# Slot lists built on the chip by one-hot matmuls instead of slot writes, gate weights stored behind each row, long runs in the conversions

## The chip, the cores and the metric

The kernel runs on one core of one Trainium2 chip. The metric is the device time of one execution in microseconds; lower is better. The core has TensorE (matmuls, "PE" in the profile, its weight loads "PEld"), VectorE ("DVE"), ScalarE ("ACT"), GpSimd ("POOL"), SyncE ("SP", which issues most transfers) and 16 DMA engines.

## The reference

Attention with a window of 64 positions over 8 batches, 8 heads and 576 positions gives 4608 rows of 512 values. Each row goes to the best two of eight experts, with weights from a softmax over noisy logits. All in f32.

```python
rel = pos[:, None] - pos[None, :]
mask = (rel >= 0) & (rel < window)
attn = softmax(np.where(mask, scale * q @ k.T, -1e9))
x = (attn @ v) as rows [N, DM]
noisy = x @ w_gate + np.log1p(np.exp(x @ w_noise)) * noise
top2 = np.argpartition(-noisy, 2, axis=1)[:, :2]
top2_w = softmax over the two
for e in range(E):
    for k in range(2):
        m = top2[:, k] == e
        h = np.maximum(x[m] @ w1[e], 0.0)
        out[m] += top2_w[m, k, None] * (h @ w2[e])
```

## The kernel before, in words

The work has two stages, and the order of the instructions on each engine is the order in which the Python code issues them (no scheduler).

**Attention, 36 tiles of 128 rows** (the loop over `j`, line 719). It is a software pipeline: in pass `j` the scores of tile `j` are multiplied (L255), ScalarE and VectorE take the window and the maximum (L275, L283, L288), GpSimd subtracts the maximum (L289, once per tile), ScalarE takes the exponential of tile `j-1` (L293), TensorE transposes it (L301), VectorE masks it (L306), TensorE multiplies tile `j-2` with the values (L324), and ScalarE scales tile `j-3` (L343), which is then stored in DRAM as rows of `xrows` (L346). SyncE loads two to three tiles ahead.

**Routing** runs beside it. The tiles are grouped in five routes (`ROUTE`, 7, 7, 7, 6 and 9 tiles). For each, `route` (L407) issues some 35 small operations, a few per pass (`RATE`): softplus, noise, the best two experts as one-hot `oh`, running counts `cum`, and by two matmuls with a triangle and with ones (L463, L464) the rank of each row in its expert's list. The rank and the expert's base give a slot number `posi` (L477).

**Slot writes.** Each expert has a list in DRAM, `slots`, of `CAP` = 1216 entries and some for an overflow. An entry is a row number and a gate weight. For each tile and each of the two choices GpSimd issues one indirect DMA (L483) that writes 128 entries of 8 bytes to the slots of `posi`, behind a memset of one element; 72 in all. They wait in a queue `slots` and are taken from it one, then one or two, in each pass. Before, SyncE has filled the lists with numbers of empty rows (`load_pads`, L175).

**Experts.** Each expert's list is cut in chunks of 384, 448 and 384 rows. The first two chunks of expert 0 start before the routing is complete (`EARLY`). A chunk's list is read back (`load_list`, `load_lists`), GpSimd gathers its rows from `xrows` by indirect DMAs (L546), and `turn` (L564) makes the transposed operand in two parts, `xh` rounded and `xl` the rest. For expert 0 TensorE transposes; for the others the rows go out to DRAM (`turn_out`) and come back per tile in another order (`turn_in`), VectorE transposes blocks of 32 (L574), and ScalarE and VectorE convert (L584, L585), reading and writing with strides. Then `up` (L609): for each of eight column blocks, four times three matmuls of 384 or 448 columns; and `down` (L645): for each 128 rows, eight times three matmuls of 512 columns, one eviction by ScalarE, scaled by the gate weight of the list (L659), and one indirect DMA that adds the rows to the output (L640). In the 448-row chunk the last 64 rows take another path (L664 to L670). `spread` (L55) sets the side work (weight splits, gathers, the next `turn`) between the matmuls.

The chunk loop is at line 785. In its first pass the rest of the routing and of the slot writes runs beside the first up- and down-projection; `catch_up` (L793) makes sure that the gather of the second chunk has been issued before its `turn`. Up to sixteen steps of the first up-projection run already in the last passes of the attention loop (`ahead`).

The program stores zeros to the whole output beforehand (`zero_out`, L195), 37 transfers of 256 KB.

Of the kernel before, what the change touches and what calls it, by code (L numbers as in the profile page):

```python
# [65 lines left out]
def tile_kernel(ctx, tc, qT, kT, vx, vT, wgx, noise, w1, w2, out):  # L66
# [97 lines left out]

    pad_s = acon.tile([128, ROWS, 2], I32)
    pad_o = acon.tile([OVT, 128, 2], I32)
    nc.gpsimd.memset(pad_s, 0)
    nc.gpsimd.memset(pad_o, 0)
    nc.gpsimd.iota(pad_s[:, :, 0], pattern=[[0, ROWS]], base=0, channel_multiplier=1)
    nc.gpsimd.iota(pad_o[:, :, 0], pattern=[[1, 32], [32, 4]], base=0, channel_multiplier=0)  # L170
    pad_f = pad_s.rearrange("c t w -> c (t w)")
# [3 lines left out]
    def load_pads(q):  # L175
        if q == 0:
            nc.sync.dma_start(rows(L, LIST * 2, [[ROWS * 2, 128], [LIST * 2, E - 1], [1, ROWS * 2]]),
                              pad_f[:, None, :].to_broadcast([128, E - 1, ROWS * 2]))
            nc.sync.dma_start(rows(L, (LIST + ROWS * 128) * 2, [[2, TAIL], [LIST * 2, E - 1], [1, 2]]),
                              pad_f[:TAIL, None, :2].to_broadcast([TAIL, E - 1, 2]))  # L180
            return
        pad_t = pad_o.rearrange("k p c -> k (p c)")
        if q == 1:
            nc.sync.dma_start(rows(L, 0, [[256, CAP // 128], [1, 256]]), pad_t[:CAP // 128])
            nc.sync.dma_start(rows(L, CAP // 128 * 256, [[256, 1], [1, CAP % 128 * 2]]), pad_t[:1, :CAP % 128 * 2])
        else:
            nc.sync.dma_start(rows(L, CAP * 2, [[256, OVT], [LIST * 2, E], [1, 256]]),
                              pad_t[:, None, :].to_broadcast([OVT, E, 256]))

    REST = [lambda: nc.sync.dma_start(noise_sb, noise), lambda: nc.sync.dma_start(X[0:DUMP, :], zero),  # L190
            lambda: load_pads(0), lambda: load_pads(1), lambda: load_pads(2)]

    blank = list(range(N // 128 + 1))
# [734 lines left out]
```

## Time and profile before

| what | us |
|---|---|
| median of 3 runs | 1135.25 |
| lowest and highest | 1126.39, 1136.22 |
| the profiled execution | 1131.99 |
| its span, first to last instruction | 1130.2 |
| TensorE busy | 1044.2 |
| VectorE busy | 469.2 |
| ScalarE busy | 437.4 |
| GpSimd busy | 338.6 |

The profile is of one execution. Busy times are sums over instructions; matmuls are pipelined and their ends modelled, so a busy TensorE need not be at its peak. An idle time is put down to what ended it: a semaphore of another engine, a DMA, or "issue", when the profile shows nothing that the engine waited for; "remote" is a release that the profile finds on none of the core's engines. "PEclk", and the column behind the engines in the windows, are TensorE's granted clock as a share of 2.4 GHz.

### The profile page before, as it was taken

To read this page: it belongs to the slowest core of one execution; us is meant where nothing else is said; L and a number is where in the kernel's file an instruction comes from. 1 tells how busy PE (TensorE), PEld (TensorE's weight loads), DVE (VectorE), ACT (ScalarE), POOL (GpSimd) and SP (SyncE) were. 2 spreads that over 40 slices of the span, in tenths; PEclk is the share of its full clock that TensorE was granted. 3 is DMA by queue.
4 is the path that set the end of the run, shared out by engine and by line. 5 is a ranking of instruction groups with operands and counts; after the bars stand their busy time and mean duration, and the time that the engine had idled before them with its cause. 6 is when DMAs were issued, how large, how long until landed. Compare 5 with 4: busy or idle time off the path is not lost. (4 is left out here: it accounts for less than half of the span.)

```text
span 1130.2 us, 19820 instructions
## 1 busy us (share of the span) xinstructions
PE 1044.2 (92%) x8025; PEld 925.7 (82%) x8025; DVE 469.2 (42%) x943; ACT 437.4 (39%) x1011; POOL 338.6 (30%) x387
## 2 busy tenths in 40 slices
PE   9788888578599999999999999999999999999996
PEld 8777777366589888898988898889888988889895
DVE  5586556324114523452263325334533452354320
ACT  4776555332123432442253335323432343253320
POOL 4345444616412222122312123212221222322121
PEclk9898888879699999999999999999999999999998
DMA  9988889537414752564447445634762564244422
GB/s 321 314 300 206 214 198 307 150 133 235 123 27 112 221 146 33 173 195 103 81 130 200 103 108 146 180 81 98 203 172 40 157 205 113 44 99 112 102 33 31
DMA packets 104519, 168.07 MB, mean 149 GB/s; under 512 B 15096, under 2 KB 50530, under 8 KB 102626
## 3 DMA queue, kind: packets, MB, share of 16 engines
q1 hardware_dynamic: 84962, 126.78, 35.3%
q0 software_dynamic: 19456, 39.93, 19.2%
q8 instruction: 65, 1.06, 0.4%
q14 instruction: 36, 0.29, 0.1%
HBM read 109.54 MB, written 57.14 MB: 147 GB/s over the span
## 5 line engine op out<-in xcount | busy, mean ns | idle before, releaser
L625 PE MATMUL ps_u<-xh,w1h 128*128 128x384 f32 (+1 forms) x752 | 261.6, 348 | 15.6 <-ACT xh L584 15.1
L640 POOL DMA_INDIRECT out_dram<-yo,lts x70 | 112.1, 1602 | 543.9 <-ACT yo L659 430.7
L626 PE MATMUL ps_u<-xl,w1h 128*128 128x384 f32 (+1 forms) x752 | 261.4, 348 | 4.5 <-DVE xl L585 4.5
L627 PE MATMUL ps_u<-xh,w1l 128*128 128x384 f32 (+1 forms) x752 | 260.3, 346 | 0.0
L654 PE MATMUL ps_d<-w2h,hh 128*128 128x512 f32 x576 | 225.3, 391 | 0.0
L656 PE MATMUL ps_d<-w2h,hl 128*128 128x512 f32 x576 | 225.2, 391 | 0.0
L655 PE MATMUL ps_d<-w2l,hh 128*128 128x512 f32 x576 | 225.0, 391 | 0.0
L632 DVE SCALAR_TENSOR_TENSOR hl<-ps_u,hh 128x384 fp32r<-128x384 f32 x188 | 104.8, 557 | 275.9 <-ACT hh L631 261.6
L631 ACT ACTIVATE hh<-ps_u 128x384 fp32r<-128x384 f32 x188 | 92.5, 492 | 246.9 <-PE ps_u L627 236.5
L625 PEld LDWEIGHTS ps_u<-xh,w1h 128*128 128x128 f32 x752 | 141.9, 189 | 23.9 <-ACT xh L584 18.7
L626 PEld LDWEIGHTS ps_u<-xl,w1h 128*128 128x128 f32 x752 | 141.9, 189 | 11.2 <-DVE xl L585 6.7
L627 PEld LDWEIGHTS ps_u<-xh,w1l 128*128 128x128 f32 x752 | 141.9, 189 | 4.0
L585 DVE TENSOR_TENSOR xl<-xy,xh 128x512 fp32r<-128x512 f32 (+1 forms) x70 | 71.5, 1021 | 150.7 <-ACT xh L584 150.7
L654 PEld LDWEIGHTS ps_d<-w2h,hh 128*128 128x128 f32 x576 | 108.6, 189 | 23.8 <-issue 1.8
L656 PEld LDWEIGHTS ps_d<-w2h,hl 128*128 128x128 f32 x576 | 108.4, 188 | 22.8
L655 PEld LDWEIGHTS ps_d<-w2l,hh 128*128 128x128 f32 x576 | 108.5, 188 | 21.9
L659 ACT ACTIVATE yo<-ps_d,lts 128x512 f32<-128x512 f32 x63 | 43.4, 690 | 160.2 <-PE ps_d L656 119.1
L324 PE MATMUL ps_o<-vw,pt 64*64 64x85 f32 x2176 | 71.0, 257 | 29.4 <-issue 22.8
L584 ACT ACTIVATE xh<-xy 128x512 fp32r<-128x512 f32 (+1 forms) x70 | 74.4, 1063 | 56.1 <-DVE xy L574 56.1
L324 PEld LDWEIGHTS ps_o<-vw,pt 64*64 64x64 f32 x2176 | 58.7, 149 | 40.3 <-issue 32.1
L483 POOL DMA_INDIRECT slots<-val,posi x72 | 70.0, 972 | 20.1 <-issue 14.7
L546 POOL DMA_INDIRECT xg<-xrows,lts x70 | 69.3, 990 | 21.4 <-issue 20.1
(149 smaller groups left out, 991.3 us busy)
## 6 DMA issues: line engine op xcount, KB each, us to landing
xs<-xg SPq DMA_DIRECT2D x63, 256.0 KB
xg<-xs SPq DMA_DIRECT2D x63, 256.0 KB
w2s<-in_w_dram SPq DMA_DIRECT2D x7, 2048.0 KB
w1s<-in_w_dram SPq DMA_DIRECT2D x7, 2048.0 KB
vw<-in_vx_dram SPq DMA_DIRECT2D x36, 272.0 KB
out_dram<-zero SPq DMA_DIRECT2D x37, 256.0 KB
qc<-in_qT_dram SPq DMA_DIRECT2D x36, 256.0 KB
KW<-in_kT_dram SPq DMA_DIRECT2D x36, 256.0 KB
```

The costliest lines, as they stand in the source:

```text
L324: nc.tensor.matmul(PO[j][u * 64:u * 64 + 64, a, g * 2 + x, :], lhsT=pt[pa, w, u * 2 + g, x * 64:x * 64 + 64], rhs=v[pa, (i + w) % 2, :, u, ...
L584: nc.scalar.activation(h, cur[q], AF.Copy)
L585: nc.vector.tensor_tensor(l, cur[q], h.bitcast(F32), op=OP.subtract)
L625: nc.tensor.matmul(p[:, :n], lhsT=w1h[:, k, fs], rhs=xh[:, k, :n], start=(k == 0), stop=False)
L626: nc.tensor.matmul(p[:, :n], lhsT=w1h[:, k, fs], rhs=xl[:, k, :n], start=False, stop=False)
L627: nc.tensor.matmul(p[:, :n], lhsT=w1l[:, k, fs], rhs=xh[:, k, :n], start=False, stop=(k == KD - 1))
L631: nc.scalar.activation(h, p[:, :main], AF.Relu)
L632: nc.vector.scalar_tensor_tensor(l, p[:, :main], 0.0, h.bitcast(F32), op0=OP.max, op1=OP.subtract)
L640: nc.gpsimd.indirect_dma_start(out=out[:DUMP + seen.get((e, c), NT) * 128], out_offset=bass.IndirectOffsetOnAxis(ap=LT[e, c][q][:m, 0:1], ...
L654: nc.tensor.matmul(p, lhsT=hh[f][:, sl], rhs=w2h[:, f, :], start=(f == 0), stop=False)
L655: nc.tensor.matmul(p, lhsT=hh[f][:, sl], rhs=w2l[:, f, :], start=False, stop=False)
L656: nc.tensor.matmul(p, lhsT=hl[f][:, sl], rhs=w2h[:, f, :], start=False, stop=(f == KF - 1))
```

## The change

1. The slot writes go, and with them the prefilled lists. Instead a route now makes, for a pair of tiles and both choices, a one-hot of the slot number's low 7 bits over 128 lanes (`ha`, four compares of 128 columns on GpSimd, or on VectorE once the attention loop is over), a one-hot of its upper part over 80 list tiles (`hc`, one compare of 320 columns on VectorE), and the product of the latter with two values, the tile's number and the lane difference (`hb`, 640 columns on GpSimd). Four bf16 matmuls (128x160) add the two one-hots' products in PSUM: each row's number lands at its slot. VectorE adds the result to `SLOT`, which stays on the chip. Three VectorE operations turn it into the gather's and the store's row numbers (`lists`).
2. The gate weights are written behind each row: `xrows` is 528 wide instead of 512, and each route stores 16 weights per row with one DMA (L478). The gather brings them along, and one small copy per tile (`gate_of`) takes the weight of the expert.
3. The rows that come back from DRAM are read in another order, in four transfers per chunk (`turn_in`), so that transposes, `xh` and `xl` have runs of 32 elements instead of strides.
4. The half tile moves from the second to the third chunk (384, 384, 448). The empty entries of odd list tiles point to a second dump region of the output, and the stores of tiles with another parity in the same chunk don't wait for each other. The zeros come from a buffer of half the width. `RATE` is 6 operations a pass up to tile 15 and then 8. The pieces of side work in the first two chunks are set anew.

The diff, cut:

```diff
-CHUNKS = (384, 384 + TAIL, 384)
+CHUNKS = (384, 384, 384 + TAIL)
-XB = 8
+XB = 4
+XW = DM + 2 * E
-RATE = ((16, 6), (21, 8), (27, 6), (99, 8))
+RATE = ((16, 6), (99, 8))
...
-        yield lambda: nc.vector.tensor_tensor(oh, oh, rks[:, None, :, :].to_broadcast([128, 2, n, E]), op=OP.mult)
-        pos, posi = new("pos", [128, 2, n]), new("posi", [128, 2, n], I32, bufs=2)
-        yield lambda: nc.vector.tensor_reduce(pos, oh, op=OP.add, axis=AX.X)
-        yield lambda: nc.vector.tensor_copy(posi, pos)
...
-        def scatter(c2, q):
-            nc.gpsimd.memset(spacer, 0.0)
-            s = nc.gpsimd.indirect_dma_start(
...
-        slots.extend(lambda c2=c2, q=q: scatter(c2, q) for q in range(n) for c2 in range(2))
+        wd = new("wd", [128, n, 2, E])
+        for k in range(2):
+            yield lambda: nc.vector.tensor_tensor(wd[:, :, k], oh[:, k], w[:, k, :, 1:2].to_broadcast(sh), op=OP.mult)
+        yield lambda: nc.vector.tensor_tensor(wd[:, :, 0], wd[:, :, 0], wd[:, :, 1], op=OP.add)
+        yield lambda: nc.sync.dma_start(rows(X, (DUMP + j0 * 128) * XW + DM, [[XW, 128], [128 * XW, n], [1, 2 * E]]),
+                                        wd.rearrange("p q k e -> p q (k e)"))
...
+        yield lambda: nc.vector.tensor_scalar(hi, pos, 1.0 / 128, -0.498046875, op0=OP.mult, op1=OP.add)
+        yield lambda: nc.vector.tensor_scalar(hi, hi, 12582912.0, -12582912.0, op0=OP.add, op1=OP.add)
+        yield lambda: nc.vector.scalar_tensor_tensor(lo, hi, -128.0, pos, op0=OP.mult, op1=OP.add)
+        yield lambda: nc.vector.tensor_scalar(mul[:, :, :, 1], lo, -1.0, row, op0=OP.mult, op1=OP.add)
+        def at_lane(q, x):
...
+            for k in range(2):
+                (nc.gpsimd if j < NT else nc.vector).tensor_scalar(AB[q][0][:, 2 * x + k], lane, lo[:, q + x, k:k + 1], None, op0=OP.is_equal)
+        def at_tile(q, m):
...
+            nc.vector.tensor_tensor(h[:, :2 * m], t[:, None, :].to_broadcast([128, 2 * m, E * NQ]),
...
+        def at_both(q, m):
...
+            nc.gpsimd.tensor_tensor(AB[q][1][:, :2 * m], AB[q, 1][:, :2 * m, None, :].to_broadcast(sh),
...
+        def place(q, m):
+            a, b = AB[q]
+            for x in range(2 * m):
+                nc.tensor.matmul(SP, lhsT=a[:, x], rhs=b[:, x].rearrange("p v t -> p (v t)"),
+                                 start=(x == 0), stop=(x == 2 * m - 1))
+            v = SLOT.rearrange("p v e q -> p (v e q)")
+            nc.vector.tensor_tensor(v, v, SP, op=OP.add)
+        last = None
+        for q in range(0, n, 2):
+            m = min(2, n - q)
+            slots.append(lambda q=q, m=m: (at_tile(q, m), at_lane(q, 0)))
+            slots.append(lambda q=q, m=m, f=last: (m > 1 and at_lane(q, 1), f and f()))
+            slots.append(lambda q=q, m=m: at_both(q, m))
+            last = lambda q=q, m=m: place(q, m)
+        slots.extend([lambda: None, last])
...
+        yield lambda: nc.vector.scalar_tensor_tensor(ii[0], j, 128.0, p, op0=OP.mult, op1=OP.add)
+        yield lambda: nc.vector.scalar_tensor_tensor(m, j, 0.0, odd[:, es, qs], op0=OP.is_gt, op1=OP.max)
+        yield lambda: nc.vector.scalar_tensor_tensor(ii[1], m, float(DUMP), ii[0], op0=OP.mult, op1=OP.add)
...
         def turn_out(q, m):
-            b[q] = dram.tile([4, 128, 128], F32, name="xs", bufs=8)
...
+            nc.sync.dma_start(b[q * 128:q * 128 + m], XG[e, c, q][:m, :DM])
-        def turn_in(q, m):
...
+        def turn_in(g):
+            if g == 0:
+                XC[e, c] = exa.tile([128, WIDE // 32, 128], F32, name="xc", bufs=1)
+            nc.sync.dma_start(XC[e, c][32 * g:32 * g + 32, :CHUNKS[c] // 32],
+                              rows(b, g * 128, [[DM, 32], [32 * DM, CHUNKS[c] // 32], [1, 128]]))
...
-            h, l = (x[:, :, q * 128:q * 128 + m].rearrange("p k (c t) -> p k c t", c=32) for x in (xh, xl))
+            h, l = (x[:, :, q * 128:q * 128 + m].rearrange("p k (t c) -> p k t c", c=32) for x in (xh, xl))
...
+        for x in added.setdefault((e, 1 - (QS[c] + q) % 2), []):
+            tc.declare_no_dep(s.ins, x.ins, reason="distinct rows")
...
-                nc.scalar.activation(y, p, AF.Copy, scale=LT[e, c][q].bitcast(F32)[:, 1:2])
+                nc.scalar.activation(y, p, AF.Copy, scale=wt[:, q:q + 1])
```

How this stands on the engines is seen at two places. The first is GpSimd in the middle of the attention tiles, where the first route's slots are made: `t` is the softmax's tile, `spacer` the memset before each write, `posi` the slot numbers. Before:

```order
L289 TENSOR_TENSOR t<-t,mx 128x512
L482 MEMSET spacer 1x1
L483 DMA slots<-val_168,posi 38400x2
L482 MEMSET spacer 1x1
L483 DMA slots<-val_168,posi 38400x2
L289 TENSOR_TENSOR t<-t,mx 128x512
```

In the changed kernel, at the same tiles (`ha` the one-hot over lanes, `hb` the product, `mul` the two values):

```order
L269 TENSOR_TENSOR t<-t,mx 128x512
L494 TENSOR_SCALAR ha<-lane,lo 128x128 x2
L505 TENSOR_TENSOR hb<-hc,mul_175 128x640
L494 TENSOR_SCALAR ha<-lane,lo 128x128 x2
L269 TENSOR_TENSOR t<-t,mx 128x512
L494 TENSOR_SCALAR ha<-lane,lo 128x128 x2
L505 TENSOR_TENSOR hb<-hc,mul_175 128x640
L269 TENSOR_TENSOR t<-t,mx 128x512
```

Between two subtractions GpSimd now computes instead of issuing indirect DMAs.

The second place is TensorE in the down-projection of the first chunk, shortly before its end, where the second chunk's rows are transposed (`ps_d` is the projection's result, `ident,xg` a transpose). Before:

```order
L654 MATMUL ps_d<-w2h,hh 128x512
L655 MATMUL ps_d<-w2l,hh 128x512
L656 MATMUL ps_d<-w2h,hl 128x512
L579 MATMUL ps_u<-ident,xg 128x128 x4
L654 MATMUL ps_d<-w2h,hh 128x512
```

In the changed kernel (`ps_g<-hb,ha` are the matmuls of the one-hots):

```order
L713 MATMUL ps_d<-w2h,hl 128x512
L511 LDWEIGHTS ha
L511 MATMUL ps_g<-hb,ha 128x160
L511 LDWEIGHTS ha
L511 MATMUL ps_g<-hb,ha 128x160
L711 MATMUL ps_d<-w2h,hh 128x512
L712 MATMUL ps_d<-w2l,hh 128x512
L713 MATMUL ps_d<-w2h,hl 128x512
L625 MATMUL ps_u<-ident,xg 128x128 x4
```

TensorE has gained five groups of such matmuls here, each of which stands in front of the projection's next matmuls and waits for VectorE's and GpSimd's one-hots.

## Rows read from the trace of the kernel before

**Rows 1.** The page's 40 slices of the span, TensorE's busy tenths:

```profile
PE   9788888578599999999999999999999999999996
```

**Rows 2.** Windows: length, busy us (instructions) of PE, PEld, DVE, ACT, POOL, clock, DMA share, GB/s:

```profile
50.00:75.00 25.00, 20.33 (x533) 18.02 (x531) 20.00 (x53) 20.13 (x72) 12.20 (x15) 0.93 0.89 316
...
85.00:160.00 75.00, 61.54 (x1268) 53.59 (x1268) 47.64 (x134) 44.00 (x156) 40.19 (x66) 0.86 0.83 212
...
212.00:237.00 25.00, 9.62 (x63) 4.85 (x54) 0.60 (x5) 0.73 (x3) 16.86 (x33) 0.57 0.12 16
...
264.00:279.00 15.00, 15.00 (x69) 12.06 (x69) 2.04 (x8) 2.58 (x4) 11.46 (x20) 0.92 0.62 189
...
279.00:294.50 15.50, 0.42 (x2) 0.00 (x0) 0.97 (x2) 1.56 (x3) 10.52 (x18) 0.65 0.25 27
```

**Rows 3.** Timeline of GpSimd: start, us, instruction, idle time before it and releaser:

```profile
50.47 1.04 POOL L289 TENSOR_TENSOR t<-t,mx 128x512 f32<-128x512 f32 x1 [1.64 <-DVE mx L288]
...
94.84 1.05 POOL L289 TENSOR_TENSOR t<-t,mx 128x512 f32<-128x512 f32 x1
...
182.14 0.96 POOL L546 DMA_INDIRECT xg<-xrows,lt  x1 [0.30 <-issue]
...
207.37 1.04 POOL L289 TENSOR_TENSOR t<-t,mx 128x512 f32<-128x512 f32 x1 [3.17 <-DVE mx L288]
...
231.46 0.96 POOL L483 DMA_INDIRECT slots<-val,posi  x1 [0.22 <-issue]
...
288.73 0.96 POOL L483 DMA_INDIRECT slots<-val,posi  x1 [0.23 <-issue]
```

**Rows 4.** Timeline of TensorE, same columns:

```profile
38.84 1.97 PE L235 MATMUL ps_g<-wgx_sb,vt 128*128 128x64 f32 x8 [3.23 <-DMA vt<-in_vT_dram]
...
182.84 0.31 PE L324 MATMUL ps_o<-vw,pt 64*64 64x85 f32 x2 [0.41 <-issue]
...
211.55 0.96 PE L324 MATMUL ps_o<-vw,pt 64*64 64x85 f32 x39
...
222.10 0.41 PE L324 MATMUL ps_o<-vw,pt 64*64 64x85 f32 x2 [1.10 <-issue]
...
237.40 0.69 PE L625 MATMUL ps_s<-xh,w1h 128*128 128x384 f32 x1 [1.17 <-DVE hl L632]
...
261.90 0.19 PE L464 MATMUL ps_g<-cum,ones_b 128*128 128x72 bf16 x1 [1.68 <-DVE cum L457]
```

**Rows 5.** Timeline of ScalarE, behind the first down-projection:

```profile
293.51 0.69 ACT L659 ACTIVATE yo<-ps_d,lt 128x512 f32<-128x512 f32 x1 [12.07 <-remote]
```

**Rows 6.** Waits of TensorE and VectorE: us in total, times, longest:

```profile
PE ps_u L625 <- ACT xh L584: 15.1, 1, 15.1
...
PE ps_u L626 <- DVE xl L585: 4.5, 7, 0.7
...
DVE t L283 <- POOL w1l L217: 4.6, 3, 1.7
```

**Rows 7.** Groups by shape: busy us, mean ns, idle time before and releaser:

```profile
L483 POOL DMA_INDIRECT slots<-val,posi x72 | 70.0, 972 | 20.1 <-issue 14.7 <-DVE val L480 5.4
...
L585 DVE TENSOR_TENSOR xl<-xy,xh 128x512 fp32r<-128x512 f32 x63 | 68.4, 1085 | 146.9 <-ACT xh L584 146.9
...
L217 POOL TENSOR_TENSOR w1l<-w1s,w1h 128x256 fp32r<-128x256 f32 x16 | 11.4, 732 | 8.6 <-ACT w1h L216 8.6
...
L669 DVE TENSOR_TENSOR yo<-yo,ps_d 64x512 f32<-64x512 f32 x8 | 5.4, 679 | 11.4 <-ACT yo L668 11.4
...
L585 DVE TENSOR_TENSOR xl<-ps_u,xh 128x512 fp32r<-128x512 f32 x6 | 4.2, 692 | 32.6 <-ACT xh L584 21.8 <-issue 10.8
```

**Rows 8.** Windows, the same columns as rows 2, during the prefill:

```profile
32.00:36.00 4.00, 3.62 (x108) 3.21 (x107) 2.28 (x5) 3.27 (x11) 2.47 (x3) 1.00 0.91 100
```

**Rows 9.** Timeline of VectorE, the last route's chain:

```profile
250.81 0.20 DVE L426 TENSOR_SCALAR a<-u 128x72 f32<-128x72 f32 x1 [0.64 <-ACT u L425]
...
261.66 0.19 DVE L457 TENSOR_TENSOR cum<-sc 128x80 bf16<-128x80 bf16 x1
```

More of the change, by code (lines that the diff above doesn't have):

```diff
@@ L139, in tile_kernel @@
     spacer = consts.tile([1, 1], F32)
-    zero = gw.tile([128, DM], F32, name="zero", bufs=1)
+    zero = gw.tile([128, DM // 2], F32, name="zero", bufs=1)
     nc.vector.memset(zero, 0.0)
@@ L162, in tile_kernel @@
         nc.gpsimd.memset(v[:, :, 4], 0.0)
[L165 to L171, printed above, removed]
-    noise_sb = consts.tile([128, NT, E], F32)
[L175 to L193, printed above, removed]
+    noise_sb = consts.tile([128, NT, E], F32)
+    REST = [lambda: nc.sync.dma_start(noise_sb, noise), lambda: nc.sync.dma_start(rows(X, 0, [[XW, DUMP], [DM // 2, 2], [1, DM // 2]]),
+                                                                          zero[:, None, :].to_broadcast([128, 2, DM // 2])),
+            lambda: nc.sync.dma_start(X[0:DUMP, DM:], zero[:, :2 * E])]
+    blank = list(range(N // 128 + 2))
     def zero_out():
@@ new lines, in tile_kernel, with lists @@
+    QS = [sum(-(-CHUNKS[d] // 128) for d in range(c)) for c in range(len(CHUNKS) + 1)]
+    def lists(es, qs, tag):
+        sh = [128, es.stop - es.start, qs.stop - qs.start]
+        pool = EXB["p"] if es.start else gw
+        ii = [pool.tile(sh, I32, name=x + tag, bufs=1) for x in ("lx", "lo")]
+        m = ii[1].bitcast(F32)
+        j, p = SLOT[:, 0, es, qs], SLOT[:, 1, es, qs]
+        yield lambda: nc.vector.scalar_tensor_tensor(ii[0], j, 128.0, p, op0=OP.mult, op1=OP.add)
+        yield lambda: nc.vector.scalar_tensor_tensor(m, j, 0.0, odd[:, es, qs], op0=OP.is_gt, op1=OP.max)
+        yield lambda: nc.vector.scalar_tensor_tensor(ii[1], m, float(DUMP), ii[0], op0=OP.mult, op1=OP.add)
+        for e in range(es.start, es.stop):
+            for c in range(len(CHUNKS)):
+                if qs.start <= QS[c] and QS[c + 1] <= qs.stop:
+                    LT[e, c] = [x[:, e - es.start, QS[c] - qs.start:QS[c + 1] - qs.start] for x in ii]
@@ L541, in tile_kernel, with first_list, other_lists @@
+    def first_list(c):
+        return lists(slice(0, 1), slice(QS[c], QS[c + 1]), f"{c}")
+    def other_lists():
+        return lists(slice(1, E), slice(0, NQ), "s")
+    GW = {}
     seen = {(0, c): j for c, j in enumerate(sorted(EARLY))}
     def gather(e, c):
+        GW[e, c] = exa.tile([128, 4], F32, name="wg", bufs=3)
         def whole(q, m):
-            XG[e, c, q] = exa.tile([128, DM], F32, name="xg", bufs=XB)
+            XG[e, c, q] = exa.tile([128, XW], F32, name="xg", bufs=XB)
@@ L551, in gather @@
[L551 removed]
+            return [lambda q=q, m=m: whole(q, m) for q, m in tiles(c)] + [lambda: None] * 2 + [
+                lambda q=q, m=m: gate_of(q, m) for q, m in tiles(c)]
+        b = dram.tile([WIDE, DM], F32, name="xs", bufs=3)
         def turn_out(q, m):
[L554 to L556 removed]
@@ L564, in turn @@
+        return ([lambda q=q, m=m, f=f: f(q, m) for f in (whole, turn_out) for q, m in tiles(c)]
+                + [lambda g=g: turn_in(g) for g in range(4)]
+                + [lambda: [gate_of(q, m) for q, m in tiles(c)]])
     def turn(e, c):
@@ L692, in drain_slots @@
     def drain_slots(n):
-        for f in slots[:n]:
-            f()
-        del slots[:n]
+        while slots and n:
+            slots.pop(0)()
+            n -= 1
     up00 = up(0, 0)
```

153 lines of the change are left out of this document (92 added, 61 removed).

## The prediction

> **What bounds the kernel now.** I read first the page's slices [rows 1]: TensorE is 9 or more tenths busy from the twelfth slice (about 311 us) to the end, so the expert stage is TensorE's own work, and time can only be won or lost in the first third. Next the table of windows [rows 2]. Two stretches stand out: 212 to 237 us, where TensorE is busy 9.6 of 25 us, VectorE 0.6 and ScalarE 0.7, while GpSimd works 16.9 us and the DMA engines are nearly idle; and 279 to 294.5 us, where TensorE does nothing and GpSimd 10.5 us. Then GpSimd's own rows in order of time [rows 3]: in both stretches it issues slot writes (L483) one after another, the last of them at 231.46 and at 288.73 us. TensorE's rows [rows 4] show a few matmuls and then a gap put down to "issue" (nothing that the profile knows of), over and over, until 237.4 us; in the second stretch ScalarE's next eviction starts only at 293.51 us, and the profile names nothing on the core for its wait ("remote") [rows 5]. Both ends lie 5 to 6 us behind the last slot write. The same gaps stand in the attention tiles wherever slot writes run, and also at 182.8 us, where the indirect DMA on GpSimd is not a slot write but a gather of whole rows [rows 3, 4]. So I take it that indirect DMAs issued by GpSimd starve the other engines of instructions, whatever they carry. Where TensorE needs few instructions per us it goes on: at 264 to 279 us, beside 11.5 us of GpSimd, it runs its 69 matmuls, most of 512 columns, without a gap, 0.22 us each [rows 2].
>
> What these writes cost in the tiles: GpSimd's subtraction L289 comes once per tile. Nine tiles almost without slot writes take 94.84 - 50.47 = 44.4 us, 4.93 each; the next 17, with them, 207.37 - 94.84 = 112.5 us, 6.62 each [rows 3].
>
> **The change, part by part.** The sum is made against the profiled execution, 1132.0 us (span 1130.2 and 1.8 around it); the median of three runs is 1135.25, 0.3% above.
>
> A. The 17 tiles. All 72 slot writes go, each 0.97 us and a memset [rows 7]. Per pair of tiles come four compares and one product on GpSimd, a compare and an addition on VectorE, four bf16 matmuls on TensorE. GpSimd: the compare has 128 columns, half of L217's 256 at 0.73 us, so 0.37 to 0.73 us; the product has 640, by L217 and L289 (0.73 and 1.04 us for 256 and 512) 1.2 us. A pair is 2.7 to 4.1 us, four pairs per seven tiles 1.5 to 2.4 us a tile, where 14 slot writes took at least 1.9: GpSimd is about as busy as before. VectorE: 320 and 160 columns, by 692 ns for 512 columns [rows 7] 0.43 and about 0.3 us, four times per seven tiles, and seven more small operations per route at about 0.23 us: (2.9 + 1.6)/7 = 0.64 us a tile. It now has 47.6/75 x 6.62 = 4.2 us a tile [rows 2], so 4.85. If VectorE could be filled, that is the period; at the 0.80 that it reaches from 50 to 75 us [rows 2] it would be 6.05. I take the middle, 5.4: 17 x (6.62 - 5.4) = -21 us. Bounds: 4.93 as without slot writes, -29 (somewhat less is possible, since tile 8 to 18 also split a weight there); 6.05, -10.
>
> B. 211.5 to 256.5 us, the end of attention and the first up-projection. Of the 25.9 us between the two rows at 211.55 and 237.40 [rows 4], TensorE's work is at most the 9.6 busy us, most of them at a clock of 0.5, so about 5 at full clock: -21 us. New on TensorE's path: the last four groups of matmuls (a 72-column one takes 0.19 us [rows 4], so at most 0.75 a group), and waits for the compares, which VectorE makes itself from here on: +4. Together -17; bounds -21 and -8 (every group waits a whole product and its compares).
>
> C. 256.5 to 294.5 us, the first down-projection. The 15.1 us wait goes [rows 6]. In its place: VectorE's chain from the softplus to the running counts takes 250.81 to 261.66 us [rows 9], and TensorE already waits 1.68 us for its end [rows 4]. The change puts 12 compares, 3 wide compares and 3 additions into it, 12 x 0.2 + 3 x 0.43 + 3 x 0.3 = 4.6 us; I count +3, since TensorE has its own new work before that point. Behind the rank matmul the first group needs about 16 small VectorE operations, four compares and a product, 3.7 + 0.8 + 1.2 = 5.7 us, against seven triples of 0.22 us matmuls, 4.6: +1. Five groups of matmuls +2.5, the last conversion before the next up-projection +1.3. Sum -15.1 + 7.8 = -7; bounds -14 (all of it beside other work) and 0.
>
> D. The prefilled slot lists go, the gate weights come. At 32 to 36 us the DMA engines are 0.91 busy and move 100 GB/s, against 316 at 50 to 75 us [rows 2, 8]: that is the prefill's 1344 pieces of 8 to 72 bytes. TensorE then waits 3.23 us for vt [rows 4], which goes. The change writes gate weights five times, 768 to 1152 pieces of 64 bytes each, four of them among the tiles. SyncE waits there for VectorE, with the loads of two tiles ahead queued behind. A dip of 4 us at a third of the rate costs some 2.7 us of DMA time; at a share of 0.83 [rows 2] there are 0.17 x 6.6 x 7 = 8 us of slack per seven tiles, so most of it is hidden; I count 0.8 for each, 4 x 0.8 - 3.2 = 0. Bounds -3 and, with nothing hidden, 4 x 2.7 - 3.2 = +8.
> The Trainium skill bears on this: DMA: Bandwidth & Descriptors, section Why small descriptors are slow (HBM only), gives a fixed cost of some three cycles per packet and 32 bytes of metadata per operation, which for 900 pieces on 16 engines is an estimated fraction of a microsecond. By it D would be -3; by the row it is anything up to +8. The row shows the larger price, and it decides.
>
> E. Expert stage. The conversions L584 and L585 read and write in long runs now: 1085 ns should become about 690 [rows 7]. TensorE only waits 4.5 us in all for them [rows 6]: -4; the rest is hidden behind matmuls. The turned rows now come in four transfers behind all of a chunk's outgoing ones instead of tile by tile; they have an up-projection to land (96 matmuls of 384 columns, about 16 us at 0.22 us for 512), and if that fails the conversions still have the 72 of the down-projection, another 16 us: 0. The parity of the accumulating stores frees GpSimd, which waits anyway: 0. The last tile is now the half tile: two short VectorE passes (0.68 us and at most as much) come behind the last matmul: +1.
>
> Sum: -21 - 17 - 7 + 0 - 4 + 1 = -48, so 1084 in the profiled execution and, with the 0.3%, 1087 beside the median.
>
> **Rivals.**
> Clean: nothing new waits. A -29, B -21, C -14, D -3, E -4, end +1: 1132 - 70 = 1062. For it: GpSimd and TensorE have room. Against: VectorE at 80% from 50 to 75 us.
> VectorE becomes the bound. It waited three times, 4.6 us in all, behind GpSimd's w1l, 16 operations, whose result it does not read [rows 6]: 0.29 us each. Some 2.9 GpSimd operations a tile then add 0.84 us: A -7 instead of -21, B -12, C -4: 1132 - 7 - 12 - 4 - 4 + 1 = 1106.
> The Trainium skill has this as a rule (SBUF — State Buffer, section Who interferes with whom): GpSimd and a VectorE operation with two SBUF inputs hold one port pair exclusively, so the later one blocks. The trace agrees in so far as three of the sixteen show a wait.
> The stalls stay. If the gaps called "issue" came from something else (zero stores, weight loads), A and B would be gone and C with its 15.1: only E and the end, and some new work beside them, 1132 - 4 + 1 + 2 = 1131. Against: from 50 to 75 us the DMA engines are 0.89 busy and GpSimd computes for 12 us, and VectorE is kept at 0.80 [rows 2]; the gaps come with the indirect DMAs.
> Slower: TensorE stands in order behind each group's matmuls, so a GpSimd that needs longer than TensorE's other work holds it. At 2.7 to 4.1 us a pair it does not. From about 6 us a pair it decides, since the eight groups of B and C follow each other at 2 to 3 us; at 10 us a pair the tiles are at 6.8 us (A +3), B is -21 + 4 x 7 = +7 and C -15 + 5 x 8 = +25: 1132 + 35 - 4 + 1 = 1164. Against it stands that GpSimd's subtraction takes 1.04 or 1.05 us in each of its rows, beside whatever else runs [rows 3].
>
> **How the numbers follow.** Forecast (1068 to 1098) 0.60; clean 0.14; VectorE the bound 0.17; stalls stay 0.04; slower 0.05. A difference of 1%, 11 us, is about what a measurement of this kernel can tell from none. Faster by more: 0.60 + 0.14 + 0.17 = 0.91; within 1%: 0.04 for the stalls that stay; slower 0.05. The range must leave out no more than 0.2: from 1055, below the clean case, to 1120, above VectorE's. Predicted 1087.
>
> **What would show it.** Right: no "issue" gaps of TensorE in the tiles past the eighteenth, a period near 5.4 us, the up-projection of the second chunk starting near 250 us instead of 294.5, and no change of length from there to the last matmul but some 4 us. Wrong: TensorE waiting for GpSimd before the new matmuls by more than 10 us in all; vt waits behind each store of gate weights; gaps of "issue" with GpSimd free of indirect DMAs.

## The result, and the profile after

The changed kernel takes 1092.91 us (median of 4 runs, 1091.35 to 1099.93), the kernel before beside it 1133.38 us (median of 4, 1126.39 to 1136.22): 0.9664 times, 95% interval 0.9601 to 0.9727. The forecast was 1087. The profiled execution has a span of 1090.4 us against 1130.2. This holds for the chip of that measurement; on another chip (12) the same two programs came out the other way round, and on two more (7 and 10) the kernel before was as fast as on that one (the first experiment). What follows keeps the two cases apart.

TensorE's slices no longer show the hole of [rows 1]:

```profile
PE   9887787779999999999999999999999999999996
```

Windows, with the columns of [rows 2]; in 212 to 237 us, where TensorE was busy 9.62 us and VectorE 0.60, TensorE now has 15.82 and VectorE 21.80 of 25:

```profile
85.00:160.00 75.00, 59.22 (x1527) 54.10 (x1518) 64.97 (x182) 50.05 (x176) 39.70 (x50) 0.93 0.80 251
212.00:237.00 25.00, 15.82 (x75) 13.02 (x75) 21.80 (x69) 4.97 (x10) 9.39 (x9) 0.86 0.49 147
237.00:256.00 19.00, 17.94 (x93) 14.45 (x93) 11.53 (x33) 3.67 (x6) 8.16 (x8) 0.91 0.81 269
```

GpSimd's subtraction (L269, before L289) of the tenth, the 19th and the last tile, to be held against 50.47, 94.84 and 207.37 in [rows 3]:

```profile
45.26 1.04 POOL L269 TENSOR_TENSOR t<-t,mx 128x512 f32<-128x512 f32 x1 [1.64 <-DVE mx L268]
...
88.69 1.05 POOL L269 TENSOR_TENSOR t<-t,mx 128x512 f32<-128x512 f32 x1 [0.47 <-DVE mx L268]
...
181.79 1.04 POOL L269 TENSOR_TENSOR t<-t,mx 128x512 f32<-128x512 f32 x1 [2.70 <-DVE mx L268]
```

TensorE in order of time. The one gap called "issue" shown is beside a gather; the rows at L511 are the one-hot matmuls and what they wait for; at 227.09 the first down-projection begins; then come the second chunk's first matmul and the last one:

```profile
164.91 0.39 PE L304 MATMUL ps_o<-vw,pt 64*64 64x85 f32 x5 [0.41 <-issue]
...
206.00 0.45 PE L511 MATMUL ps_g<-hb,ha 128*128 128x160 bf16 x4 [2.56 <-DVE d L390]
...
218.41 0.45 PE L511 MATMUL ps_g<-hb,ha 128*128 128x160 bf16 x4 [1.91 <-DVE SLOT L514]
...
223.72 0.72 PE L511 MATMUL ps_g<-hb,ha 128*128 128x160 bf16 x4 [3.77 <-DVE SLOT L514]
...
227.09 0.40 PE L711 MATMUL ps_d<-w2h,hh 128*128 128x512 f32 x1
...
236.95 0.49 PE L511 MATMUL ps_g<-hb,ha 128*128 128x160 bf16 x4 [1.89 <-POOL hb L505]
...
251.60 0.33 PE L675 MATMUL ps_u<-xh,w1h 128*128 128x384 f32 x1
...
1079.89 0.40 PE L722 MATMUL ps_d<-w2l,ht 128*128 128x512 f32 x1
```

In the kernel before, the first matmul of the first down-projection, the second chunk's first and the last one:

```profile
256.55 0.39 PE L654 MATMUL ps_d<-w2h,hh 128*128 128x512 f32 x1
...
294.52 0.74 PE L625 MATMUL ps_u<-xh,w1h 128*128 128x448 f32 x1 [15.10 <-ACT xh L584]
...
1118.88 0.39 PE L656 MATMUL ps_d<-w2h,hl 128*128 128x512 f32 x1
```

These rows give the stages, as differences of start times: to the 19th tile 94.8 us before and 88.7 after; the 17 tiles 112.5 and 93.1; from the last subtraction to the second chunk's first matmul 87.2 and 69.8; from there to the last matmul 824.4 and 828.3; the rest of the span 11.3 and 10.5. In all -39.8 us: -6.1, -19.4, -17.3, +3.9, -0.8.

TensorE's waits (total, times, longest), which answer to [rows 6]: the wait of 15.1 is gone, the one for `xl` fell from 4.5 to 1.4, and waits for the slot sums and the one-hots are new:

```profile
PE ps_g L215 <- DVE SLOT L514: 8.0, 3, 2.7
PE ps_g L511 <- DVE SLOT L514: 5.7, 2, 3.8
PE ps_g L511 <- POOL hb L505: 4.8, 4, 1.9
PE ps_o L304 <- issue: 3.6, 6, 1.3
...
PE ps_u L676 <- DVE xl L631: 1.4, 7, 0.2
```

Groups by shape; the conversion L631 takes 693 ns where L585 took 1085 [rows 7]:

```profile
L631 DVE TENSOR_TENSOR xl<-xy,xh 128x512 fp32r<-128x512 f32 x63 | 43.7, 693 | 108.0 <-ACT xh L630 108.0
...
L505 POOL TENSOR_TENSOR hb<-hc,mul 128x640 bf16<-128x640 bf16 x16 | 21.9, 1368 | 26.1 <-DVE hc L499 19.5 <-DVE ha L494 5.9 <-PE ps_g L511 0.7
```

### The profile page after: what moved, and what is told of

The parts are those of the page before. It is cut to its first block, busy times and chain, and to the rows that moved or that the text cites. A ratio compares the mean times of both kernels' runs of the same rounds, so it can differ in the third digit from the quotient of the medians.

```text
span 1090.4 us, 20135 instructions
## 1 busy us (share of the span) xinstructions
PE 1029.2 (94%) x8097; PEld 912.9 (84%) x8097; DVE 486.5 (45%) x1144; ACT 404.8 (37%) x1011; POOL 317.9 (29%) x383
## 4 chain that ended last, share of the span: by engine, by line
PE 78%; DVE 10%; issue 4%; ACT 3%; POOL 2%; DMA 1%; SPq 1%; POOLq 0%; ACTq 0%; DVEq 0%
PE ps_u L676 13%; PE ps_u L677 13%; PE ps_u L675 13%; PE ps_d L711 11%; PE ps_d L712 11%; PE ps_d L713 11%; PE ps_o L304 2%; DVE pt L286 1%; DVE t L263 1%; DVE mx L268 1%; PE ps_s L245 1%; DVE xl L631 1%; PE ps_g L215 1%; ACT xh L630 1%; DMA vt<-in_vT_dram 1%
## 5 line engine op out<-in xcount | busy, mean ns | idle before, releaser
L693 POOL DMA_INDIRECT out_dram<-yo,los x70 | 114.8, 1641 | 543.5 <-ACT yo L716 520.7
L711 PE MATMUL ps_d<-w2h,hh 128*128 128x512 f32 x576 | 229.0, 398 | 0.0
L681 ACT ACTIVATE hh<-ps_u 128x384 fp32r<-128x384 f32 x188 | 92.5, 492 | 255.5 <-PE ps_u L677 248.5
L716 ACT ACTIVATE yo<-ps_d,wg 128x512 f32<-128x512 f32 x72 | 49.6, 688 | 222.2 <-issue 114.6
L712 PEld LDWEIGHTS ps_d<-w2l,hh 128*128 128x128 f32 x576 | 108.9, 189 | 23.4
L711 PEld LDWEIGHTS ps_d<-w2h,hh 128*128 128x128 f32 x576 | 108.6, 188 | 23.1
L631 DVE TENSOR_TENSOR xl<-xy,xh 128x512 fp32r<-128x512 f32 x70 | 46.6, 666 | 122.5 <-ACT xh L630 122.5
L586 POOL DMA_INDIRECT xg<-xrows,lxs x70 | 71.1, 1015 | 21.3 <-issue 18.6
L323 ACT ACTIVATE x<-ps_o,r 128x80 f32<-128x80 f32 x288 | 67.0, 347 | 13.0 <-DVE r L315 10.2
L630 ACT ACTIVATE xh<-xy 128x512 fp32r<-128x512 f32 x70 | 42.4, 606 | 71.4 <-DVE xy L619 71.3
L269 POOL TENSOR_TENSOR t<-t,mx 128x512 f32<-128x512 f32 x36 | 37.7, 1047 | 87.9 <-DVE mx L268 69.5
L304 PE MATMUL ps_o<-vw,pt 64*64 64x85 f32 x2176 | 54.2, 247 | 8.3 <-issue 3.6
```

The costliest lines, as they stand in the source:

```text
L304: nc.tensor.matmul(PO[j][u * 64:u * 64 + 64, a, g * 2 + x, :], lhsT=pt[pa, w, u * 2 + g, x * 64:x * 64 + 64], rhs=v[pa, (i + w) % 2, :, u, ...
L323: nc.scalar.activation(XT[j][:, :, a * 4 + k], o[:, k, :, 0:16], AF.Copy, scale=r[:, k:k + 1])
L586: nc.gpsimd.indirect_dma_start(out=XG[e, c, q][:m], out_offset=None, in_=X[:DUMP + seen.get((e, c), NT) * 128], in_offset=bass.IndirectOff ...
L681: nc.scalar.activation(h, p[:, :main], AF.Relu)
L693: s = nc.gpsimd.indirect_dma_start(out=out[:(2 + seen.get((e, c), NT)) * 128], out_offset=bass.IndirectOffsetOnAxis(ap=LT[e, c][1][:m, q:q ...
L711: nc.tensor.matmul(p, lhsT=hh[f][:, sl], rhs=w2h[:, f, :], start=(f == 0), stop=False)
```

## The experiments

They ran in five jobs, each on whichever chip it was given: chip 10 (32-byte shift, writes put back, writes left out, product on VectorE), 12 (the two kernels again), 7 (distances, later softmax, earlier place, all in one), 12 (one operation), 5 (distances undone). The kernel before ran beside each of them, and its medians there were 1073.9, 1072.6, 1073.4, 1074.5 and 1133.6 us (12, 15, 17, 11 and 17 runs).

**The two kernels again.** The surprise of the first job, told first since all the rest hangs on it.

> The kernel before, unchanged, with a profile. In the first job its runs beside the variants took 1074 us, where the runs that the prediction was made from took 1126 to 1136. If the slot writes cost less there (the DMA or GpSimd side of that chip or session serves them faster), the profile shows the writes (L483) without issue gaps of TensorE and 17 tiles of about 5 us each, and about 1074 us. If the two groups of runs differ in something else (the expert stage, the clock), the tiles still take 6.6 us and the gap lies elsewhere. If it is 1126 to 1136 us again, the first job's figure belongs to that job alone.

> The changed kernel, unchanged, in the same job as the kernel before. If the low time of the kernel before comes from a chip on which everything runs faster, this one is faster than 1093 us by as much (about 1035 us). If only the slot writes are cheaper there, it stays at 1090 to 1097 us, and is slower than the kernel before by 15 to 25 us there.

Measured on chip 12: 1073.06 us for the kernel before, 1096.56 us for the changed one, which is 1.0211 times the kernel before (1.0176 to 1.0246): slower there. The kernel before again, TensorE and GpSimd in the stretch that had the gaps (at 217.59 the first down-projection begins), and its windows (at 212 to 237 us it is already further on in the program):

```profile
196.47 1.41 PE L324 MATMUL ps_o<-vw,pt 64*64 64x85 f32 x64
...
217.59 0.39 PE L654 MATMUL ps_d<-w2h,hh 128*128 128x512 f32 x1
...
240.72 0.47 PE L625 MATMUL ps_u<-xh,w1h 128*128 128x448 f32 x1 [1.05 <-ACT xh L584]
```

```profile
100.20 1.04 POOL L289 TENSOR_TENSOR t<-t,mx 128x512 f32<-128x512 f32 x1 [0.66 <-DVE mx L288]
...
191.80 1.04 POOL L289 TENSOR_TENSOR t<-t,mx 128x512 f32<-128x512 f32 x1 [3.35 <-DVE mx L288]
...
196.83 0.96 POOL L483 DMA_INDIRECT slots<-val,posi  x1 [0.23 <-issue]
```

```profile
85.00:160.00 75.00, 60.73 (x1501) 55.52 (x1505) 52.66 (x146) 48.19 (x173) 43.69 (x70) 0.91 0.88 232
...
212.00:237.00 25.00, 22.01 (x108) 18.03 (x107) 14.13 (x45) 9.09 (x19) 13.31 (x21) 1.00 0.73 205
```

The write takes the same 0.96 us, and beside it TensorE runs 64 of the matmuls of [rows 4] in 1.41 us without a gap. So the instruction alone doesn't make the gaps. TensorE's waits called "issue" before these matmuls, in the first measurement and then on chip 12:

```profile
PE ps_o L324 <- issue: 22.8, 52, 1.3
```

```profile
PE ps_o L324 <- issue: 15.5, 12, 4.4
```

They don't vanish on chip 12, but they are fewer and lie elsewhere: of all idle times of TensorE over 0.3 us that are put down to "issue", 45 of 55 overlap an indirect DMA in the first measurement and 3 of 15 on chip 12. "Gaps" means from here on those beside indirect DMAs. Chip 5 shows them again (the counterpart run with the distances undone; this is the kernel before but for an unused buffer, which moves the lines by one):

```profile
220.48 0.36 PE L325 MATMUL ps_o<-vw,pt 64*64 64x85 f32 x4 [1.07 <-issue]
...
221.90 0.41 PE L325 MATMUL ps_o<-vw,pt 64*64 64x85 f32 x2 [1.06 <-issue]
```

```profile
212.00:237.00 25.00, 10.46 (x82) 6.83 (x81) 3.89 (x17) 2.97 (x11) 20.70 (x39) 0.62 0.26 70
```

Stage by stage, from the same four start times (us):

| | to tile 19 | 17 tiles | to 2nd chunk | to last matmul | rest | span |
|---|---|---|---|---|---|---|
| before, first chip | 94.8 | 112.5 | 87.2 | 824.4 | 11.3 | 1130.2 |
| before, chip 12 | 100.2 | 91.6 | 48.9 | 821.5 | 11.8 | 1074.1 |
| after, first chip | 88.7 | 93.1 | 69.8 | 828.3 | 10.5 | 1090.4 |
| after, chip 12 | 95.5 | 92.9 | 69.6 | 828.4 | 10.4 | 1096.8 |
| writes left out, chip 10 | 96.9 | 79.7 | 50.7 | 821.9 | 11.9 | 1061.1 |
| distances, chip 7 | 94.4 | 92.5 | 69.0 | 818.4 | 10.9 | 1085.2 |
| all in one, chip 7 | 95.3 | 92.6 | 57.5 | 821.5 | 10.8 | 1077.8 |

The changed kernel hardly differs between the chips; the kernel before loses 21 us in the tiles and 38 us behind them on the chips with gaps. Part of this is TensorE's clock, which from 85 to 160 us is granted at 0.86 with the gaps and at 0.91 on chip 12; its share was not told apart. Against the kernel before on chip 12 the changed one wins 4.7 us up to the 19th tile and loses 1.3 us in the 17 tiles, 20.7 us on the way to the second chunk and 6.9 us in the expert stage.

What makes the chips differ is open: the packets and bytes of each queue, those that bring instructions among them, are the same in both profiles of the kernel before. Only chip 12 was met in two jobs, so that for the others the chip and the session on it can't be told apart.

**The writes left out.** Edit, in the kernel before:

```diff
-        slots.extend(lambda c2=c2, q=q: scatter(c2, q) for q in range(n) for c2 in range(2))
```

> The kernel before with its 72 slot writes left out and nothing in their place: the lists keep their prefilled padding, so the rows that the experts gather and add are padding rows. It tells what the writes cost by themselves. Theory: without them the tiles take 4.9 us instead of 6.6 (-29 us), the end of attention and the first up-projection lose about 21 us and the first down-projection 15 us: 1133 - 65 = 1068 us, some 25 us below the changed kernel, which pays for its one-hots. Rival (the gaps called issue come from something else): 1120 us or more.

Measured on chip 10: 1062.93 us, 0.9913 times the kernel before there (0.9883 to 0.9944). The time is near the theory's 1068, but it comes from 1074 and not from 1133. Where these gaps are missing, the 72 writes cost 11 us, and they cost it in the tiles (79.7 us against 91.6 on chip 12; behind them 50.7 against 48.9). On a chip with gaps this kernel wasn't run, so that there the writes alone make the gaps is argued from where these lie, and not shown. Against this row of the table the changed kernel on chip 12 takes 13 us more in the tiles and 19 us more to the second chunk, the places of its one-hots, and 6.5 us more in the expert stage, where the distances of the operands account for it (below).

**The writes put back** beside the one-hots. Edit, in the changed kernel, four such entries per pair of tiles:

```diff
+            s = nc.gpsimd.indirect_dma_start(out=L,
+                out_offset=bass.IndirectOffsetOnAxis(ap=posi[:, q, c2:c2 + 1], axis=0),
+                in_=val[:, c2, q, :], in_offset=None)
```

> The changed kernel with the 72 slot writes put back beside the one-hots, into a list that nothing reads. Theory (indirect DMAs of GpSimd starve the engines of instructions): TensorE's waits put down to issue go from 5.6 us to 30 us or more, the 17 tiles from 5.1 us each back to 6.6 us or more (+25 us), and the end of attention grows by 10 to 25 us: 1128 to 1143 us. Rival (the one-hots' VectorE work is the bound now, and the writes lie beside it): at most +5 us, 1098 us.

Measured on chip 10: 1133.54 us (1.0556, 1.0518 to 1.0594). The time that the theory gave, and not for its reason: "issue" before the matmuls with the values (L304) is 5.9 us, none of it beside a write, and TensorE waits for GpSimd, which has about 1.25 us of write behind each step of the one-hots:

```profile
PE ps_g L523 <- POOL spacer L494: 32.6, 11, 4.3
...
PE ps_o L304 <- issue: 5.9, 4, 2.7
```

This is the mechanism of the prediction's rival "slower", seen where it was provoked.

**A shift of 32 bytes.** Edit: `name="wg", bufs=3` becomes `bufs=4`.

> The changed kernel with a fourth buffer of the gate-weight tile, which does nothing but move every tile behind it by 32 bytes. In the expert stage the down-projection's 512-column matmuls start every 227 ns (median) in the kernel before and every 231 ns in the changed one, in every chunk, the last one too, where no rows are gathered; the tiles they read begin at 32 modulo 64 bytes before and at 0 modulo 64 now. Theory (place of the operands in memory): with 32 modulo 64 again the pitch is 227 ns; 4 ns times about 1850 matmuls is 7 us, so about 1086 us, and 821 us instead of 828.3 from the second chunk's first matmul to the last one. Rival (wider rows, four transfers or other traffic beside the matmuls): pitch stays 231 ns and the time 1093 us.

Measured on chip 10: 1095.05 us (1.0199, 1.0173 to 1.0225), the 512-column pitch (from start to start) 231 ns: the place modulo 64 isn't it. Nor is it the moving tile's place alone: `w2h` lies in this program where it lies in the kernel before, modulo 1024 bytes.

**The distances of the operands.** Edit:

```diff
-        GW[e, c] = exa.tile([128, 4], F32, name="wg", bufs=3)
+        GW[e, c] = exa.tile([128, 4], F32, name="wg", bufs=8)
+    gw.tile([128, 32], F32, name="shift", bufs=1)
```

> The changed kernel with two unused buffers (160 bytes ahead of the rows' tiles, 128 bytes ahead of w2h) and nothing else; they give the tiles that TensorE reads the same distances modulo 512 bytes as in the kernel before (moving w2h to stationary hh 256, moving xh to stationary w1h 0 and 256; in the changed kernel 384, 352 and 480). The 32-byte shift left the 512-column pitch at 231 ns, but it left the distance of hh to w2h as it was. Theory (the distance of the two operands): pitch 227 ns again and 7 us less than the changed kernel, 1086 to 1090 us. Rival (something else in the program): pitch 231 ns, 1093 to 1097 us.

Measured on chip 7: 1086.17 us (1.0092, 1.0056 to 1.0128). The first and the 49th matmul of the last chunk's down-projection, in the kernel before (10.93 us apart, 227.7 ns each), in the changed kernel (11.12 us, 231.7 ns) and in this one (10.90 us, 227.1 ns):

```profile
1102.74 0.39 PE L654 MATMUL ps_d<-w2h,hh 128*128 128x512 f32 x1
...
1113.67 0.39 PE L654 MATMUL ps_d<-w2h,hh 128*128 128x512 f32 x1
```

```profile
1059.73 0.40 PE L711 MATMUL ps_d<-w2h,hh 128*128 128x512 f32 x1
...
1070.85 0.40 PE L711 MATMUL ps_d<-w2h,hh 128*128 128x512 f32 x1
```

```profile
1054.51 0.40 PE L712 MATMUL ps_d<-w2h,hh 128*128 128x512 f32 x1
...
1065.41 0.39 PE L712 MATMUL ps_d<-w2h,hh 128*128 128x512 f32 x1
```

The stretch to the last matmul falls by 10.0 us, from 828.4 to 818.4: some 1,780 matmuls of the down-projections at 4 ns are 7 us; those of the up-projections with 384 columns start every 173.6 ns instead of 175.0 (means), an estimated 3 us over some 2,200.

**The distances undone in the kernel before.** Edit: the second line of the last diff alone, in the kernel before.

> The counterpart of place512: the kernel before with one unused 128-byte buffer ahead of w2h, which turns the distance from stationary hh (its first half) to moving w2h from 256 to 384 modulo 512 bytes, the changed kernel's value, and that of one of the two xh tiles to w1h from 256 to 384. Theory (the distance of the two operands sets the pitch): the 512-column pitch goes from 227 to about 231 ns and the stretch from the second chunk's first matmul to the last one from 821.5 to about 827 us; 1.005 to 1.007 times the kernel before. Rival (place512's gain had another source): 227 ns and the same time.

Measured on chip 5, where the kernel before takes 1133.64 us: 1143.22 us (1.0071, 1.0034 to 1.0109), the stretch to the last matmul 831.4 us, where the first measurement has 824.4. The same two matmuls, 11.05 us apart, 230.2 ns each:

```profile
1115.58 0.39 PE L655 MATMUL ps_d<-w2h,hh 128*128 128x512 f32 x1
...
1126.63 0.40 PE L655 MATMUL ps_d<-w2h,hh 128*128 128x512 f32 x1
```

Both directions agree: unused buffers alone are worth 1.2% of this kernel (two of them) and 0.7% (one). Two things qualify the theory. Counted as for `xh`, from the stationary tile to the moving one, `w2h` lies at 128 in the changed kernel and at 384 here, 128 bytes the other way round; both expectations call the changed kernel's value 384. And a matmul's own distance doesn't decide alone. Half of these matmuls are at distance 0 in all four programs, and they start every 226.7 ns (mean) in the kernel before and in the one with the distances put back, but every 229.4 ns in the two others; the other half goes from 227.6 or 227.7 to 232.8 ns.

**The product on VectorE behind the tiles.** Edit: `nc.gpsimd.tensor_tensor(AB[q][1]...` becomes `(nc.gpsimd if j < NT else nc.vector).tensor_tensor(AB[q][1]...`.

> The changed kernel with the one-hots' product on VectorE instead of GpSimd once the last tile is past. From 182 to 252 us seven VectorE operations that overlap a GpSimd product take 7 us longer in all than the same operations elsewhere. Theory (a GpSimd product holds VectorE back): these 7 us go, eight products of 0.5 to 0.9 us come, TensorE waits less for sums and products: 1088 to 1091 us. Rival (VectorE is full there and any work more on it is on the path): 5 us slower, 1098 us.

Measured on chip 10: 1093.34 us (1.0174, 1.0145 to 1.0203). The way to the second chunk is 67.2 us instead of 69.6, and the lengthened VectorE operations there go from 7.1 to 0.7 us, but TensorE now waits 7.1 us for VectorE's product, where it waited 4.8 us for GpSimd's; the gain of some 2 us isn't resolved by the times alone.

**The last route's softmax later.** Edit:

```diff
-                side += [lambda: (drain(2), drain_slots(1))] * 2 + [w]
+                side += [lambda: (len(pending) > 1 and drain(2), drain_slots(1))] * 2 + [w]
```

> The changed kernel, but in the first up-projection the last route's softmax and rank work waits until the route before it is done with; it then runs in the first down-projection and behind it. Theory (at the end of attention VectorE is the bound, 21.8 of 25 us busy from 212 to 237 us, and TensorE stands behind it in the places of the one-hots): some 16 operations of 0.2 us and their order leave the path, the stretch from the 36th tile's subtraction to the second chunk's first matmul shrinks from 69.7 us by 5 to 10 us: 1084 to 1091 us. Rival (GpSimd's product decides there, or the work only comes back in the next projection): within 2 us of 1093 to 1097 us.

Measured on chip 7: 1094.96 us (1.0183, 1.0142 to 1.0224). Both are partly right: the way to the second chunk shrinks from 69.6 to 62.1 us, and the stretch to the last matmul grows from 828.4 to 833.4, since the next up-projection now takes 22 us instead of 17. VectorE's work was moved, not removed.

**The one-hot work earlier in the tile.** Edit: one `drain_slots(1)` moves from behind `soft_max2` to ahead of `drain(rate(0))`.

> The changed kernel with one of the two places per tile at which one-hot work is issued moved from behind the row maximum to the front of the tile. TensorE waits 8.0 us (three times) at the logits and 5.7 us (twice) at the one-hots for the addition of the slot sums, which stands in VectorE's queue behind the tile's predicated copy and maximum. Theory (it is the place in the queue): these waits go, the 17 tiles take 5.0 us instead of 5.3: 1085 to 1090 us. Rival (VectorE is full in these tiles, so a wait only moves): within 2 us of 1093 to 1097 us.

Measured on chip 7: 1093.13 us (1.0153, 1.0113 to 1.0193); the 17 tiles take 93.0 us as before, 5.47 each (this expectation and that of the writes put back set out from 5.3 and 5.1). The wait of the logits for the sums is gone, and the one-hot matmuls wait 6.9 us for GpSimd's product (4.8 in the changed kernel) and 6.3 us for ScalarE's copy of the logits (2.8): the rival, a wait that only moves.

```profile
PE ps_g L511 <- POOL hb L505: 6.9, 5, 2.5
PE ps_g L511 <- ACT vw L221: 6.3, 5, 1.7
```

**All in one.**

> All of it in one: the two unused buffers, the later softmax of the last route, the earlier place of the one-hot work, and the product on VectorE behind the last tile. If each of the four theories holds, 7 + 7 + 6 + 2 = 22 us less than the changed kernel: 1072 to 1076 us, no slower than the kernel before where that takes 1073 us. If they share one bound (VectorE), 10 us: 1084 to 1087 us.

Measured on chip 7: 1074.57 us, 1.001 times the kernel before (0.9984 to 1.0036). Most of the 22 us that were expected is seen in the table: against the changed kernel on chip 12 the second chunk comes 12 us sooner behind the tiles, and the stretch to the last matmul is 7 us shorter. The earlier place of the one-hot work added nothing to it (92.6 us for the 17 tiles). It needs no slot writes, so it has nothing that the gaps could come with but gathers and stores; on a chip with gaps it wasn't tried. No version here that does all of the work is faster than the kernel before on chips without gaps.

**Compare and product as one GpSimd operation**, on top of it. Edit:

```diff
+                    nc.gpsimd.tensor_scalar(AB[q][1][:, 2 * x + k, v], t, hi[:, q + x, k:k + 1],
+                                            mul[:, q + x, k, v:v + 1], op0=OP.is_equal, op1=OP.mult)
```

> As best1, and in the tiles the wide compare (VectorE) and the product (GpSimd, two inputs) are one operation: per route entry and value a compare with a scalar times a scalar over 80 columns on GpSimd, eight per pair. Theory (VectorE sets the 17 tiles' length, and a GpSimd operation with two inputs holds it back): VectorE loses 4/7 of 0.48 us a tile and the holds of 4.6 us in 17 tiles, so 5.45 us a tile becomes about 4.9 and the time 1065 us. Rival (GpSimd, whose subtraction stands in the same queue as the compares, becomes the bound: 4 x 0.6 + 8 x 0.45 us a pair): 5.5 to 6.5 us a tile, 1075 to 1092 us.

Measured on chip 12: 1089.46 us (1.0149, 1.0107 to 1.019), 6.04 us a tile. The rival: the subtraction stands behind 5 us of compares, each of 80 columns (compare and product in one) no shorter than one of 128:

```profile
L501 POOL TENSOR_SCALAR hb<-tl,hi,mul 128x80 bf16<-128x80 f32 x72 | 45.1, 637 | 0.0
...
L495 POOL TENSOR_SCALAR ha<-lane,lo 128x128 bf16<-128x128 f32 x34 | 20.4, 608 | 0.1
```

## Why the prediction was right, and where not

The sum came within 6 us of the measured time, and part of that is luck: B with C missed by +6.7 us and E by +7.9, while D missed by 6.1 the other way. It is luck too that the chip of the measurement was one with gaps, as in the trace that the sum was made from.

A, the 17 tiles: right, 5.48 us a tile against 5.4, -19.4 against -21. VectorE, the bound that was named, is busy 64.97 of 75 us, which is 0.87, between the 0.80 and the full use between which the forecast took the middle. That it sets the period is argued: the one run that took work off it in the tiles gave that work to GpSimd, which then took longer.

B and C, the end of attention and the first chunk: mis-sized. They were to bring -24 together and brought -17.3. Their border, the start of the first down-projection, is at 256.55 us before and 227.09 now; by it, counted from the last subtraction, B brought -3.9 instead of -17, outside its bounds, and C -13.5 instead of -7. The terms for what goes are right: on chip 12 the kernel before has 25.8 us for B and 23.1 for C where it had 49.2 and 38.0, which is -23.4 and -14.9 for the forecast's -21 and -15.1. The terms that failed are those for the new work: against these 25.8 and 23.1 us the changed kernel takes 45.3 and 24.5, so +19.5 in B instead of "+4" and +1.4 in C instead of "+7.8". Some of this is work that only moved: the last route's chain now ends in the up-projection. In the rows at L511 shown above TensorE stands 8.2 us in B (2.56 + 1.91 + 3.77) and 1.9 us in C, and at smaller ones between them. The forecast left VectorE 12 compares, three wide ones and three additions there, but not the eight splits of `w2` (0.68 us each) that the same passes issue, nor GpSimd's hold on them. VectorE's rows, then GpSimd's:

```profile
211.77 1.48 DVE L197 TENSOR_TENSOR w2l<-w2s,w2h 128x512 fp32r<-128x512 f32 x1
...
214.37 0.68 DVE L197 TENSOR_TENSOR w2l<-w2s,w2h 128x512 fp32r<-128x512 f32 x1
...
221.08 1.74 DVE L197 TENSOR_TENSOR w2l<-w2s,w2h 128x512 fp32r<-128x512 f32 x1
```

```profile
211.45 1.26 POOL L505 TENSOR_TENSOR hb<-hc,mul 128x640 bf16<-128x640 bf16 x1 [5.90 <-DVE ha L494]
...
220.91 1.36 POOL L505 TENSOR_TENSOR hb<-hc,mul 128x640 bf16<-128x640 bf16 x1 [3.54 <-DVE hc L499]
```

A split that begins inside a product ends behind it and takes 1.48 or 1.74 us; alone it takes 0.68. Over all VectorE operations that overlap a GpSimd one, against the shortest fifth of their own kind, this is 4.6 us in the tiles past 94 us and 7.1 us between them and 252 us. So the rival "VectorE becomes the bound" had its mechanism right, at a price of about 0.27 us a tile instead of 0.84, and the experiment with the product on VectorE shows that the tail's part is real and mostly not on the path.
The Trainium skill (SBUF — State Buffer, section Who interferes with whom) says that a VectorE operation with two SBUF inputs and a GpSimd one that reads SBUF block each other; the trace agrees for GpSimd's two-input products.

D, prefill and gate weights: 0 was forecast, bounds -3 and +8; the way to the 19th tile is 6.1 us shorter, outside the bounds (4.7 on chip 12). Of this, 5.2 us are there by the tenth tile (50.47 to 45.26), where the prefill stood, so it seems to have cost more than the one wait of 3.23 us at its end. No run leaves it out alone; over all profiles the tenth tile comes at 47.9 to 50.5 us in the four with the prefill and at 44.2 to 48.4 in the ten without it. The term "0.8 for each" store of gate weights was too high: only one wait for `vt` follows any of them, 0.53 us:

```profile
175.81 1.10 PE L215 MATMUL ps_g<-wgx_sb,vt 128*128 128x64 f32 x8 [0.53 <-DMA vt<-in_vT_dram]
```

The Trainium skill (DMA: Bandwidth & Descriptors, section Why small descriptors are slow (HBM only)), set aside for the row, would have come nearer for the 64-byte pieces, since by the prediction's estimate from it they cost a fraction of a microsecond and D was -3.

E, the expert stage: -4 was forecast, +3.9 measured. The conversions did what was said (693 ns against 690 forecast, the waits 3.1 us less). The step that failed is a term that the sum didn't have: the distances between TensorE's operands changed with the new buffers, which cost 10.0 us by the run that put them back. With them put back the stretch is 818.4 us, 3.1 less than in the kernel before on chip 12, near the -4. Nothing in the prediction looked at where the tiles lie. The end, forecast at +1, was -0.8.

The theory of the gaps: the gaps beside the slot writes went, and with them about the time that the prediction gave them, on the chip of the measurement. That indirect DMAs starve the other engines "whatever they carry" is borne out only by small gaps beside gathers (three of 0.31 to 0.41 us, the last, at 164.91, as the gather ends); the changed kernel's profile on chip 12 has none. The missing rival is that the gaps depend on the chip: on chip 12 the two stretches are without them, and by its times so is the kernel before on chips 7 and 10, and the same sum, A to E, then starts from 1074 us and ends 2% higher.

## What to carry to other kernels

A stall put down to "issue" is a property of a run until the same program has been profiled on a second chip; a change that lives from it should be judged there too, and with the cost of what replaces it measured by leaving the old work out. When a new term is put on an engine that others wait for, add up everything that the same passes issue on it, and what the neighbour engine's two-input operations hold back. When buffers are added ahead of matmul operands, compare the matmul pitch before and after: an unused buffer can be worth as much as a wait.

## What the runs showed of the hardware that was not expected

The same program takes 1070 to 1081 us on three chips (55 runs) and 1123 to 1139 us on another (17 runs), as in the first measurement; its two profiles differ in TensorE's gaps beside GpSimd's indirect DMAs, not in the duration of these DMAs (0.96 us) nor in the number of packets.

The pitch of 512-column f32r matmuls is 227 or 231 ns by where the moving and the stationary operand's tiles lie to each other (256 and 0 bytes modulo 512 against 128 or 384 and 0), moved in both directions by unused buffers alone. The matmuls at distance 0 are slower beside the others too, so what about the place does it is open. The Trainium skill (SBUF — State Buffer, section Who interferes with whom) gives TensorE two independent read ports, by which the distance would change nothing; the measurement decides. Which distances are bad in general was not tried either.

On GpSimd a compare over 128 columns takes 0.61 us, a compare and product over 80 columns 0.64 us.
